# Linear attention and channel mix on one core: q transposed by DMA instead of PE, a v cast moved to ScalarE, a two-term mix rewritten as a difference, a factor moved into a relu, and loads gated

## The chip, the cores and the metric

The kernel runs on one core of a Trainium2 chip. The metric is device time in microseconds (us) per execution. Most executions of one kernel agree within about one per cent; a run over 1.5% above the fastest of its kernel is called slow and is left out of the comparisons. All profile readings are of one execution per kernel. PE is the matmul engine, PEld its weight load, DVE the VectorE, ACT the ScalarE, POOL the GpSimd; SP only issues DMAs here.

## The reference, cut to what matters

```python
# q, k, v: (8 batches, 8 heads, 576 rows, 64)
q_s = softmax(q, axis=-1)                    # over the head dimension
k_s = softmax(k, axis=2)                     # over the sequence
kv  = einsum('bhsd,bhse->bhde', k_s, v)
x   = einsum('bhsd,bhde->bhse', q_s, kv)     # then heads joined: (8, 576, 512)
x_prev = x shifted by one row, zero first
xk = mu_k * x + (1 - mu_k) * x_prev
xr = mu_r * x + (1 - mu_r) * x_prev
out = sigmoid(xr @ w_r) * (relu(xk @ w_k)**2 @ w_v)
```

## The kernel before: the parts that matter

The work comes in two interleaved streams. `attention(b, g)` handles one half batch (four heads) and leaves `xk` and `xr` for it; there are 16 half batches. `unit(n)` handles 384 rows of the channel mix: 32 matmuls `kfp` (with wk), then three times four `rp` (with wr) and eight `vp` (with wv); there are 12 units. A scheduler has fixed the order of each engine's instructions at build time, so it need not be the order of the source. In the traces below, work that is ready stands behind an earlier instruction of the same engine that still waits (13.7 us of PE's idle time before 44.0 us come from one such case on DVE).

```python
def emit_weights():                       # POOL issues these; the DMA casts f32 to bf16
    ...                                   # wk in four loads, wr in four
    for h in range(2):                    # wv in two, halved in place by DVE
        nc.gpsimd.dma_start(out=wv_h, in_=ap)
        nc.vector.tensor_scalar(out=wv_h, in0=wv_h, scalar1=0.5, scalar2=None, op0=ALU.mult)

def attention(b, g):
    nc.gpsimd.tensor_copy(out=vv[...], in_=t[:, 2, ...])          # v cast on POOL
    for i in (1, 0):                                              # exp of k, then of q
        nc.scalar.activation(out=eqk[:, i, ...], in_=t[:, i, ...], func=ACT.Exp)
    nc.vector.reduce_sum(out=rsum[:], ...); nc.vector.reciprocal(out=rrec[:], ...)
    nc.vector.tensor_tensor(out=qs[...], in0=eq, in1=rrec..., op=ALU.mult)   # normalised q
    ...                                   # kvp: 18 matmuls; w: scaled and masked kv
    for j in range(J):                    # J = 9
        nc.tensor.transpose(out=qtp[:, j // 8, j % 8, :], in_=qs[:, j, :], identity=ident[:])
    nc.vector.tensor_copy(out=qt[...], in_=qtp[...])              # PSUM to SBUF
    for hf in range(2):
        ...                               # xp: two matmuls of w with qt
        nc.scalar.copy(out=xb[:, hf, ...], in_=xp[...])
    nc.vector.tensor_copy(out=xb[:, :, 1:64], in_=xb[:, :, 576:639])   # the shifted column
    for m, dst in enumerate((xk, xr)):
        for hf in range(2):
            nc.vector.tensor_scalar(out=xm[:, hf, :], in0=xb[now], scalar1=mu[...], op0=ALU.mult)
            nc.vector.tensor_scalar(out=xq[:, hf, :], in0=xb[prev], scalar1=om[...], op0=ALU.mult)
        nc.vector.tensor_tensor(out=dst[...], in0=xm[:], in1=xq[:], op=ALU.add)
```

(Access patterns and some arguments are cut, marked by `...`.)

The softmax here doesn't subtract the row's maximum and nothing guards it: scores larger than these inputs give would overflow.

Of the kernel before, what the change touches and what calls it, by code (L numbers as in the profile page):

```python
# [8 lines left out]
ACT = mybir.ActivationFunctionType  # L9
ALU = mybir.AluOpType  # L10
AX = mybir.AxisListType

F32 = mybir.dt.float32
BF16 = mybir.dt.bfloat16


@with_exitstack
def kernel(
# [18 lines left out]
    nc = tc.nc  # L37

    B, H, S, D = q.shape
# [18 lines left out]

    raw = {}

    def emit_load(b: int, g: int):
        t = ldpool.tile([128, 3, 2, J * D], F32, tag="raw", name="raw")
        for i, src in enumerate((q, k, v)):
            ap = bass.AP(tensor=src.tensor,
                         offset=src.offset + (b * H + 4 * g) * S * D,
                         ap=[[J * D, 128], [2 * S * D, 2], [1, J * D]])
            nc.sync.dma_start(out=t[:, i, :, :], in_=ap)
        raw[b, g] = t

    mu_sb = const.tile([8, 128], F32, name="mu_sb")  # L70
    for m, src in enumerate((moe_mu_k, moe_mu_r)):
        for g in range(2):
# [1 line left out]
                         ap=[[64, 2], [128, 2], [1, 64]])  # L74
            nc.scalar.dma_start(out=mu_sb[4 * m + 2 * g:4 * m + 2 * g + 2, :]
                                .rearrange("p (u e) -> p u e", u=2), in_=ap)
    emit_load(0, 0)
    emit_load(0, 1)


# [18 lines left out]
    wv_bf = const.tile([128, FT, C], BF16, name="wv_bf")  # L99
    wr_bf = const.tile([128, CT, C], BF16, name="wr_bf")  # L100

    def emit_weights():
        for dst, src, n in ((wk_bf, moe_w_k, F), (wr_bf, moe_w_r, C)):
            for g in range(2):
                for u in range(2):
                    ap = bass.AP(tensor=src.tensor,
                                 offset=src.offset + (4 * g + 2 * u) * D * n,
                                 ap=[[n, 64], [D * n, 2], [1, n]])
                    nc.gpsimd.dma_start(out=dst[64 * u:64 * u + 64, 2 * g:2 * g + 2, :],
                                        in_=ap)  # L110
        for h in range(2):
            n = FT // 2
            ap = bass.AP(tensor=moe_w_v.tensor,
                         offset=moe_w_v.offset + h * n * 128 * C,
                         ap=[[C, 128], [128 * C, n], [1, C]])
            wv_h = wv_bf[:, h * n:(h + 1) * n, :]
            nc.gpsimd.dma_start(out=wv_h, in_=ap)
            nc.vector.tensor_scalar(out=wv_h, in0=wv_h, scalar1=0.5, scalar2=None,  # L118
                                    op0=ALU.mult)

    mu = const.tile([128, 8], F32, name="mu")
    om = const.tile([128, 8], F32, name="om")

    def emit_mu():
        mup = psum.tile([128, 8], F32, tag="mm", bufs=4, name="mup")
        nc.tensor.transpose(out=mup[:], in_=mu_sb[:], identity=identf[:])
        nc.vector.tensor_copy(out=mu[:], in_=mup[:])
        nc.vector.tensor_scalar(out=om[:], in0=mup[:], scalar1=-1.0, scalar2=1.0,
                                op0=ALU.mult, op1=ALU.add)


    xpair = {}
# [2 lines left out]
    def attention(b: int, g: int):  # L135
        t = raw.pop((b, g))
        vv = vvs[box[0] % 3]
        xb = xbs[box[0] % 3]
        box[0] += 1
        if b // 2 not in xpair:  # L140
            xpair[b // 2] = (xpool.tile([128, CT, 2 * S], BF16, tag="xk", name="xk"),
                             xpool.tile([128, CT, 2 * S], BF16, tag="xr", name="xr"))
        xk, xr = xpair[b // 2]
        c0 = S * (b % 2)

        nc.gpsimd.tensor_copy(out=vv[:, :, 0:128].rearrange("p j (u d) -> p j u d", u=2),  # L146
                              in_=t[:, 2, :, :].rearrange("p u (j d) -> p j u d", d=D))
        eqk = apool.tile([128, 2, J, 2, D], BF16, tag="eqk", name="eqk")
        for i in (1, 0):
            nc.scalar.activation(  # L150
                out=eqk[:, i, :, :, :],
                in_=t[:, i, :, :].rearrange("p u (j d) -> p j u d", d=D),
                func=ACT.Exp)
        eq = eqk[:, 0, :, :, :].rearrange("p j u d -> p (j u) d")
        rsum = apool.tile([128, 2 * J], F32, tag="rsum", name="rsum")
        nc.vector.reduce_sum(out=rsum[:], in_=eq, axis=AX.X)  # L156
        rrec = apool.tile([128, 2 * J], F32, tag="rrec", name="rrec")
        nc.vector.reciprocal(out=rrec[:], in_=rsum[:])
        qs = apool.tile([128, J, 128], BF16, tag="qs", name="qs")
        nc.vector.tensor_tensor(out=qs[:].rearrange("p j (u d) -> p (j u) d", u=2),  # L160
                                in0=eq, in1=rrec[:, :, None].to_broadcast((128, 2 * J, D)),
                                op=ALU.mult)
        yield
        kvp = psum.tile([128, 2, 512], F32, tag="att", bufs=2, name="kvp")
        for j in range(J):
            for hf in range(2):
                r = slice(64 * hf, 64 * hf + 64)
                nc.tensor.matmul(kvp[:, hf, 0:129],  # L168
                                 lhsT=eqk[r, 1, j, :, :].rearrange("p u d -> p (u d)"),
                                 rhs=vv[r, j, 0:129], start=(j == 0), stop=(j == J - 1))  # L170
        rz = apool.tile([128, 2], F32, tag="rz", name="rz")
        nc.vector.reciprocal(out=rz[:], in_=kvp[:, :, 128])
        w = apool.tile([128, 2, 128], BF16, tag="w", name="w")
        for hf in range(2):
            nc.vector.scalar_tensor_tensor(out=w[:, hf, :], in0=kvp[:, hf, 0:128],  # L175
                                           scalar=rz[:, hf:hf + 1], in1=mask[:],
                                           op0=ALU.mult, op1=ALU.mult)
        yield
        qtp = psum.tile([128, 2, 8, 128], BF16, tag="att", bufs=2, name="qtp")
        qt = apool.tile([128, 2, S], BF16, tag="qt", name="qt")  # L180
        for j in range(J):
            nc.tensor.transpose(out=qtp[:, j // 8, j % 8, :], in_=qs[:, j, :],  # L182
                                identity=ident[:])
        nc.vector.tensor_copy(  # L184
            out=qt[:, :, :].rearrange("p h (j c) -> p j h c", c=64),
            in_=qtp[:].rearrange("p a j c -> p (a j) c")[:, 0:J, :]
            .rearrange("p j (h c) -> p j h c", h=2))
        yield
        for hf in range(2):
            xp = psum.tile([128, 2, 512], F32, tag="att", bufs=2, name="xp")  # L190
            for a in range(2):
                nc.tensor.matmul(xp[:, a, 0:288], lhsT=w[:, hf, :],  # L192
                                 rhs=qt[:, hf, 288 * a:288 * a + 288],
                                 start=True, stop=True)
            nc.scalar.copy(out=xb[:, hf, 64:64 + S].rearrange("p (a c) -> p a c", a=2),
                           in_=xp[:, :, 0:288])
            if hf == 0:
                yield
        nc.vector.tensor_copy(out=xb[:, :, 1:64], in_=xb[:, :, 64 + 512:64 + 512 + 63])
        yield  # L200
        for m, dst in enumerate((xk, xr)):
            xm = apool.tile([128, 2, S], BF16, tag="xm", name="xm")
            xq = apool.tile([128, 2, S], BF16, tag="xq", name="xq")
            for hf in range(2):
                c = 4 * m + 2 * g + hf
                nc.vector.tensor_scalar(out=xm[:, hf, :], in0=xb[:, hf, 64:64 + S],  # L206
                                        scalar1=mu[:, c:c + 1], scalar2=None, op0=ALU.mult)
                nc.vector.tensor_scalar(out=xq[:, hf, :], in0=xb[:, hf, 0:S],  # L208
                                        scalar1=om[:, c:c + 1], scalar2=None, op0=ALU.mult)
            nc.vector.tensor_tensor(out=dst[:, 2 * g:2 * g + 2, c0:c0 + S],  # L210
                                    in0=xm[:], in1=xq[:], op=ALU.add)
            yield


    def unit(n: int):
# [3 lines left out]
        for fc in range(FT):  # L219
# [3 lines left out]
                                 rhs=xk[:, ct, c0:c0 + U],  # L223
                                 start=(ct == 0), stop=(ct == CT - 1))
            rel = mpool.tile([128, U], BF16, tag="rel", bufs=3, name="rel")
            nc.scalar.activation(out=rel[:], in_=kfp[:, 0:U], func=ACT.Relu)  # L226
            nc.vector.tensor_tensor(out=k2[:, fc, :], in0=rel[:], in1=rel[:], op=ALU.mult)
            yield
        for m in range(U // 128):
# [24 lines left out]
            pass  # L254


    a0 = attention(0, 0)
    next(a0)
    a1 = attention(0, 1)
    next(a1)  # L260
    emit_weights()
    emit_mu()
    emit_load(1, 0)
    emit_load(1, 1)
    for gen in (a0, a1):
        drain(gen)

    def attention_of(batches):
        for b in batches:
            for g in range(2):  # L270
                if b + 1 < B:
                    emit_load(b + 1, g)
                yield from attention(b, g)

    ASTEPS = 16
# [45 lines left out]
```

## Time and profile before

The median is 246.6 us over three runs. The profiled execution has a span of 244.5 us.

| stretch (us) | what bounds it | sign in the profile |
|---|---|---|
| 20 to 44 | DVE's order, waiting for wv | PE 3.3 us busy of 24, DVE 10.2, DMA share 1.11 |
| 45 to 190 | DVE | DVE busy 141.4 of 145 us, PE 130.9 |
| 190 to 244.5 | PE | attention is over; a unit is 12.95 us of back-to-back matmuls |

From the page of the kernel before, the busy time per engine, and the rows of the table of 40 equal slices (each digit is a busy share in tenths):

```profile
PE 190.5 (78%) x1296; PEld 103.2 (42%) x1313; DVE 186.2 (76%) x434; ACT 120.0 (49%) x197; POOL 33.8 (14%) x32
PE   0335200898987969797979999979999999999992
DVE  1489312999999999999999999999969844252521
DMA  6999999921997587898881303203113031322313
```

PE has a hole in slices 5 to 7, while the DMA engines are full. From there on DVE is at 9 for most of the way; PE reaches a steady 9 only when DVE drops.

The chain of waits of the kernel before, the pieces around that hole (columns: start in us, us, what):

```profile
13.97 2.21 POOL vv_104 L146
...
16.72 2.37 POOL wr_bf L109 x4
19.09 0.70 POOL wv_bf L117
19.79 21.27 DMA wv_bf<-in_moe_w_v_dram
41.09 0.69 DVE wv_bf L118
...
43.28 0.68 DVE xk L210
44.00 3.49 PE kfp L222 x11
```

Read it backwards: the first `kfp` matmuls that need the second half of batch 0 wait for `xk`; the mix that makes it is queued on DVE behind the halving of wv; that waits 21 us for wv to land; and POOL issued wv only from 19.1 us on, because v casts stand in front of it in POOL's order (experiments 7 and 9 test both steps).

The timeline of the kernel before beside one v cast, from DVE and from POOL:

```profile
21.59 0.36 DVE L206 TENSOR_SCALAR xm<-xb_102,mu 128x576 bf16<-128x576 bf16 x1
21.87 1.25 DVE L208 TENSOR_SCALAR xq<-xb_102,om 128x576 bf16<-128x576 bf16 x1
...
21.68 1.28 POOL L146 CAST vv_108<-raw 128x1152 bf16<-128x1152 f32 x1 [1.08 <-DMA raw<-in_v_dram]
```

A DVE scaling of this shape takes 0.36 us and, beside a POOL cast, 1.25 us.

### The profile page before, as it was taken

How to read it: one execution, taken by the hardware profiler on the slowest of the kernel's cores; microseconds unless marked ns; L12 is line 12 of the kernel's file. 1: busy time of each engine (PE TensorE's matmuls, PEld its weight loads, DVE VectorE, ACT ScalarE, POOL GpSimd, SP SyncE). 2: the span in 40 equal slices, each digit the busy share in tenths (PEclk: the TensorE clock that was granted, in tenths of full speed). 3: DMA queues.
4: the chain of work that ended last, by engine and by line, in shares of the span. 5: the costliest groups of instructions: out<-in, count | busy, mean ns of one | idle time of the engine just before them, and what ended most of it. 6: DMA issues, size and time to landing. Idle time of an engine off the chain costs nothing.

```text
span 244.5 us, 3656 instructions
## 1 busy us (share of the span) xinstructions
PE 190.5 (78%) x1296; PEld 103.2 (42%) x1313; DVE 186.2 (76%) x434; ACT 120.0 (49%) x197; POOL 33.8 (14%) x32
## 2 busy tenths in 40 slices
PE   0335200898987969797979999979999999999992
PEld 0223200453543545453544555534655545454540
DVE  1489312999999999999999999999969844252521
ACT  4351520495292755465383774741734626162620
POOL 2375011610112010110110140100000000000000
PEclk9999655699999999999999999999999999999997
DMA  6999999921997587898881303203113031322313
GB/s 224 368 319 314 298 293 357 394 86 25 254 333 292 130 315 230 252 298 268 260 285 44 86 3 79 51 4 86 43 39 92 0 90 43 73 55 51 81 43 86
DMA packets 21065, 40.60 MB, mean 166 GB/s; under 512 B 2104, under 2 KB 3640, under 8 KB 21048
## 3 DMA queue, kind: packets, MB, share of 16 engines
q1 hardware_dynamic: 18816, 37.76, 49.4%
q0 software_dynamic: 2208, 2.62, 6.1%
q8 instruction: 10, 0.16, 0.3%
q14 instruction: 7, 0.06, 0.1%
q10 hardware_dynamic: 24, 0.00, 0.0%
HBM read 33.56 MB, written 9.44 MB: 176 GB/s over the span
## 4 chain that ended last, share of the span: by engine, by line
PE 49%; DVE 27%; DMA 14%; ACT 4%; POOL 2%; issue 1%; DVEq 0%; ACTq 0%
PE vp L239 21%; PE kfp L222 14%; PE rp L232 9%; DMA wv_bf<-in_moe_w_v_dram 9%; DVE qs L160 5%; DVE xq L208 4%; DMA raw<-in_v_dram 4%; DVE xm L206 3%; PE xp L192 2%; DVE xr L210 2%; DVE xk L210 2%; DVE rsum L156 2%; DVE ot L242 2%; ACT eqk L150 2%; PE qtp L182 2%; DMA raw<-in_q_dram 2%
## 5 line engine op out<-in xcount | busy, mean ns | idle before, releaser
L222 PE MATMUL kfp<-xk,wk_bf 128*128 128x384 bf16 x384 | 69.4, 331 | 15.9 <-DVE xk L210 15.1
L226 ACT ACTIVATE rel<-kfp 128x384 bf16<-128x384 f32 x96 | 46.1, 495 | 38.0 <-PE kfp L222 32.5
L222 PEld LDWEIGHTS <-wk_bf 128*128 128x128 bf16 x384 | 37.3, 99 | 40.0 <-issue 16.9
L150 ACT ACTIVATE eqk<-raw 128x1152 bf16<-128x1152 f32 x32 | 36.7, 1163 | 34.5 <-DMA raw<-in_q_dram 15.1
L242 DVE SCALAR_TENSOR_TENSOR ot<-th,vp 128x512 f32<-128x512 f32 x36 | 24.5, 684 | 21.7 <-PE vp L239 18.6
L235 ACT ACTIVATE th<-rp 128x512 f32<-128x512 f32 x36 | 21.6, 599 | 33.8 <-PE rp L232 33.5
L232 PE MATMUL rp<-wr_bf,xr 128*128 128x512 bf16 x130 | 36.4, 379 | 0.7
L156 DVE TENSOR_REDUCE rsum<-eqk 128x18 f32<-128x1152 bf16 x16 | 21.5, 1345 | 8.5 <-ACT eqk L150 8.5
L160 DVE TENSOR_TENSOR qs<-eqk,rrec 128x1152 bf16<-128x1152 bf16 x16 | 21.6, 1351 | 0.1
L192 PE MATMUL xp<-qt,w 128*128 128x288 bf16 x64 | 12.1, 295 | 10.2 <-DVE qt L184 6.8
L232 PEld LDWEIGHTS <-xr 128*128 128x128 bf16 x144 | 13.7, 98 | 13.3
L182 PE MATMUL qtp<-ident,qs 128*128 128x128 bf16 x144 | 11.6, 231 | 5.0 <-DVE qs L160 4.8
L146 POOL CAST vv_100<-raw 128x1152 bf16<-128x1152 f32 x6 | 8.2, 1371 | 49.3 <-PE kvp L168 42.2
L146 POOL CAST vv_108<-raw 128x1152 bf16<-128x1152 f32 x5 | 10.8, 2164 | 27.6 <-PE kvp L168 16.9
L168 PEld LDWEIGHTS <-eqk 64*128 64x128 bf16 x288 | 9.6, 102 | 11.0 <-issue 5.1
L146 POOL CAST vv_104<-raw 128x1152 bf16<-128x1152 f32 x5 | 7.7, 1547 | 44.3 <-DMA raw<-in_v_dram 22.8
L182 PEld LDWEIGHTS <-qs 128*128 128x128 bf16 x144 | 9.4, 103 | 9.5 <-DVE qs L160 7.6
L192 PEld LDWEIGHTS <-w 128*128 128x128 bf16 x64 | 6.2, 98 | 17.1 <-DVE w L175 7.4
L210 DVE TENSOR_TENSOR xr<-xm,xq 128x1152 bf16<-128x1152 bf16 x16 | 12.7, 794 | 0.0
L210 DVE TENSOR_TENSOR xk<-xm,xq 128x1152 bf16<-128x1152 bf16 x16 | 12.1, 754 | 0.0
L184 DVE COPY qt<-qtp 128x1152 bf16<-128x1152 bf16 x16 | 12.0, 747 | 0.0
L118 DVE TENSOR_SCALAR wv_bf<-wv_bf 128x2048 bf16<-128x2048 bf16 x2 | 1.4, 694 | 13.1 <-DMA wv_bf<-in_moe_w_v_dram 13.1
(78 smaller groups left out, 244.8 us busy)
## 6 DMA issues: line engine op xcount, KB each, us to landing
raw<-in_q_dram SPq DMA_DIRECT2D x16, 576.0 KB, 7.6
raw<-in_k_dram SPq DMA_DIRECT2D x16, 576.0 KB, 7.9
raw<-in_v_dram SPq DMA_DIRECT2D x16, 576.0 KB, 8.5
out_dram<-ot SPq DMA_DIRECT2D x72, 128.0 KB, 2.4
wk_bf<-in_moe_w_k_dram POOLq DMA_DIRECT2D x4, 256.0 KB, 6.8
wv_bf<-in_moe_w_v_dram POOLq DMA_DIRECT2D x2, 512.0 KB, 18.9
wr_bf<-in_moe_w_r_dram POOLq DMA_DIRECT2D x4, 128.0 KB, 8.8
mu_sb<-in_moe_mu_k_dram ACTq DMA_DIRECT2D x2, 1.0 KB
```

The source lines that it names most:

```text
L146: nc.gpsimd.tensor_copy(out=vv[:, :, 0:128].rearrange("p j (u d) -> p j u d", u=2), in_=t[:, 2, :, :].rearrange("p u (j d) -> p j u d", d=D))
L150: nc.scalar.activation(out=eqk[:, i, :, :, :], in_=t[:, i, :, :].rearrange("p u (j d) -> p j u d", d=D), func=ACT.Exp)
L156: nc.vector.reduce_sum(out=rsum[:], in_=eq, axis=AX.X)
L160: nc.vector.tensor_tensor(out=qs[:].rearrange("p j (u d) -> p (j u) d", u=2), in0=eq, in1=rrec[:, :, None].to_broadcast((128, 2 * J, D)), ...
L182: nc.tensor.transpose(out=qtp[:, j // 8, j % 8, :], in_=qs[:, j, :], identity=ident[:])
L192: nc.tensor.matmul(xp[:, a, 0:288], lhsT=w[:, hf, :], rhs=qt[:, hf, 288 * a:288 * a + 288], start=True, stop=True)
L210: nc.vector.tensor_tensor(out=dst[:, 2 * g:2 * g + 2, c0:c0 + S], in0=xm[:], in1=xq[:], op=ALU.add)
L222: nc.tensor.matmul(kfp[:, 0:U], lhsT=wk_bf[:, ct, fc * 128:(fc + 1) * 128], rhs=xk[:, ct, c0:c0 + U], start=(ct == 0), stop=(ct == CT - 1))
L226: nc.scalar.activation(out=rel[:], in_=kfp[:, 0:U], func=ACT.Relu)
L232: nc.tensor.matmul(rp[:], lhsT=xr[:, ct, c0 + 128 * m:c0 + 128 * m + 128], rhs=wr_bf[:, ct, :], start=(ct == 0), stop=(ct == CT - 1))
L239: nc.tensor.matmul(vp[:], lhsT=k2[:, ft, 128 * m:128 * m + 128], rhs=wv_bf[:, ft, :], start=(ft == 0), stop=(ft == FT - 1))
L242: nc.vector.scalar_tensor_tensor(out=ot[:], in0=th[:], scalar=1.0, in1=vp[:], op0=ALU.add, op1=ALU.mult)
```

## The change

Five things are changed. The normalised q goes through a DMA transpose, which frees PE of 144 transposes and DVE of 16 copies out of PSUM. The v cast goes from POOL to ACT. The mix is written as x_prev + mu * (x - x_prev), with `om` gone. The 0.5 of wv becomes a factor sqrt(0.5) in the relu's scale, which the square turns into 0.5. One weight load is made to wait for the first raw loads; the q loads of batch 1's two half batches wait for wk and for wr, and that of batch 2's first half for wv (this last line is not in the cut below).

```diff
+HALF_ROOT = 0.5 ** 0.5
-    def emit_load(b: int, g: int):
+    def emit_load(b: int, g: int, gate=None):
...
-            nc.sync.dma_start(out=t[:, i, :, :], in_=ap)
+            ld = nc.sync.dma_start(out=t[:, i, :, :], in_=ap)
+            after(ld, gate)          # ld waits for the DMA `gate`
+            gate = None              # so only the q load is gated
...
-            nc.vector.tensor_scalar(out=wv_h, in0=wv_h, scalar1=0.5, ...)
...
-        nc.gpsimd.tensor_copy(out=vv[...], in_=t[:, 2, ...])
-        for i in (1, 0):
+        for i in (0, 1):
             nc.scalar.activation(out=eqk[:, i, ...], ..., func=ACT.Exp)
+        nc.scalar.copy(out=vv[...], in_=t[:, 2, ...])
...
-        for j in range(J):
-            nc.tensor.transpose(out=qtp[...], in_=qs[:, j, :], identity=ident[:])
-        nc.vector.tensor_copy(out=qt[...], in_=qtp[...])
+        qt = apool.tile([128, J, 128], BF16, tag="qt", name="qt")
+        nc.sync.dma_start_transpose(out=qt[:], in_=qs[:].rearrange("p j c -> p (j c)"))
...
-            for a in range(2):       # xp in two matmuls of 288 columns
+            for c, e in ((0, 8), (8, J)):      # now 512 and 64 columns
...
+        nc.vector.tensor_tensor(out=xd[:], in0=xb[now], in1=xb[prev], op=ALU.subtract)
...
-                xm = x * mu ; xq = x_prev * om        # two tensor_scalar
+                xm = xd * mu                          # one
-            dst = xm + xq
+            dst = xm + x_prev
...
-            nc.scalar.activation(out=rel[:], in_=kfp[:, 0:U], func=ACT.Relu)
+            nc.scalar.activation(out=rel[:], in_=kfp[:, 0:U], func=ACT.Relu, scale=HALF_ROOT)
...
+    wdone = emit_weights(first)      # its first weight load waits for raw v of half batch (0,0)
+    emit_load(1, 0, wdone[3])        # behind wk
+    emit_load(1, 1, wdone[7])        # behind wr
```

(The lines of the mix are abbreviated, and the comments are added here.)

More of the change, by code (lines that the diff above doesn't have):

```diff
@@ L59, with after @@
     raw = {}
-    def emit_load(b: int, g: int):
+    SYNC = mybir.DependencyInfo(mybir.DependencyClass.Sync, mybir.DependencyReason.DATA)
+    def after(later, earlier):
+        if earlier is not None:
+            tc.add_manual_dep(later.ins, earlier.ins.name, SYNC)
+    def emit_load(b: int, g: int, gate=None):
         t = ldpool.tile([128, 3, 2, J * D], F32, tag="raw", name="raw")
@@ L66, in emit_load @@
                          ap=[[J * D, 128], [2 * S * D, 2], [1, J * D]])
-            nc.sync.dma_start(out=t[:, i, :, :], in_=ap)
+            ld = nc.sync.dma_start(out=t[:, i, :, :], in_=ap)
+            after(ld, gate)
+            gate = None
         raw[b, g] = t
+        return ld
     mu_sb = const.tile([8, 128], F32, name="mu_sb")
@@ L76 @@
                                 .rearrange("p (u e) -> p u e", u=2), in_=ap)
-    emit_load(0, 0)
+    first = emit_load(0, 0)
     emit_load(0, 1)
@@ L100, with emit_weights @@
     wr_bf = const.tile([128, CT, C], BF16, name="wr_bf")
-    def emit_weights():
+    def emit_weights(gate):
+        done = []
         for dst, src, n in ((wk_bf, moe_w_k, F), (wr_bf, moe_w_r, C)):
@@ L108, in emit_weights @@
                                  ap=[[n, 64], [D * n, 2], [1, n]])
-                    nc.gpsimd.dma_start(out=dst[64 * u:64 * u + 64, 2 * g:2 * g + 2, :],
-                                        in_=ap)
+                    done.append(nc.gpsimd.dma_start(
+                        out=dst[64 * u:64 * u + 64, 2 * g:2 * g + 2, :], in_=ap))
+                    after(done[-1], gate)
+                    gate = None
         for h in range(2):
@@ L116, in emit_weights @@
             wv_h = wv_bf[:, h * n:(h + 1) * n, :]
-            nc.gpsimd.dma_start(out=wv_h, in_=ap)
-            nc.vector.tensor_scalar(out=wv_h, in0=wv_h, scalar1=0.5, scalar2=None,
-                                    op0=ALU.mult)
+            done.append(nc.gpsimd.dma_start(out=wv_h, in_=ap))
+        return done
     mu = const.tile([128, 8], F32, name="mu")
-    om = const.tile([128, 8], F32, name="om")
     def emit_mu():
@@ L127, in emit_mu @@
         nc.vector.tensor_copy(out=mu[:], in_=mup[:])
-        nc.vector.tensor_scalar(out=om[:], in0=mup[:], scalar1=-1.0, scalar2=1.0,
-                                op0=ALU.mult, op1=ALU.add)
     xpair = {}
@@ L144, in attention @@
         c0 = S * (b % 2)
-        nc.gpsimd.tensor_copy(out=vv[:, :, 0:128].rearrange("p j (u d) -> p j u d", u=2),
-                              in_=t[:, 2, :, :].rearrange("p u (j d) -> p j u d", d=D))
         eqk = apool.tile([128, 2, J, 2, D], BF16, tag="eqk", name="eqk")
-        for i in (1, 0):
+        for i in (0, 1):
             nc.scalar.activation(
@@ L153, in attention @@
                 func=ACT.Exp)
+        nc.scalar.copy(out=vv[:, :, 0:128].rearrange("p j (u d) -> p j u d", u=2),
+                       in_=t[:, 2, :, :].rearrange("p u (j d) -> p j u d", d=D))
         eq = eqk[:, 0, :, :, :].rearrange("p j u d -> p (j u) d")
@@ L178, in attention @@
         yield
-        qtp = psum.tile([128, 2, 8, 128], BF16, tag="att", bufs=2, name="qtp")
-        qt = apool.tile([128, 2, S], BF16, tag="qt", name="qt")
-        for j in range(J):
-            nc.tensor.transpose(out=qtp[:, j // 8, j % 8, :], in_=qs[:, j, :],
-                                identity=ident[:])
-        nc.vector.tensor_copy(
-            out=qt[:, :, :].rearrange("p h (j c) -> p j h c", c=64),
-            in_=qtp[:].rearrange("p a j c -> p (a j) c")[:, 0:J, :]
-            .rearrange("p j (h c) -> p j h c", h=2))
+        qt = apool.tile([128, J, 128], BF16, tag="qt", name="qt")
+        nc.sync.dma_start_transpose(out=qt[:], in_=qs[:].rearrange("p j c -> p (j c)"))
         yield
         for hf in range(2):
-            xp = psum.tile([128, 2, 512], F32, tag="att", bufs=2, name="xp")
-            for a in range(2):
-                nc.tensor.matmul(xp[:, a, 0:288], lhsT=w[:, hf, :],
-                                 rhs=qt[:, hf, 288 * a:288 * a + 288],
+            xp = psum.tile([128, 1024], F32, tag="att", bufs=2, name="xp")
+            for c, e in ((0, 8), (8, J)):
+                nc.tensor.matmul(xp[:, 64 * c:64 * e], lhsT=w[:, hf, :],
+                                 rhs=qt[:, c:e, 64 * hf:64 * hf + 64],
                                  start=True, stop=True)
-            nc.scalar.copy(out=xb[:, hf, 64:64 + S].rearrange("p (a c) -> p a c", a=2),
-                           in_=xp[:, :, 0:288])
+            nc.scalar.copy(out=xb[:, hf, 64:64 + S], in_=xp[:, 0:S])
             if hf == 0:
@@ L200, in attention @@
         yield
+        xd = apool.tile([128, 2, S], BF16, tag="xd", name="xd")
+        nc.vector.tensor_tensor(out=xd[:], in0=xb[:, :, 64:64 + S], in1=xb[:, :, 0:S],
+                                op=ALU.subtract)
         for m, dst in enumerate((xk, xr)):
             xm = apool.tile([128, 2, S], BF16, tag="xm", name="xm")
-            xq = apool.tile([128, 2, S], BF16, tag="xq", name="xq")
             for hf in range(2):
                 c = 4 * m + 2 * g + hf
-                nc.vector.tensor_scalar(out=xm[:, hf, :], in0=xb[:, hf, 64:64 + S],
+                nc.vector.tensor_scalar(out=xm[:, hf, :], in0=xd[:, hf, :],
                                         scalar1=mu[:, c:c + 1], scalar2=None, op0=ALU.mult)
-                nc.vector.tensor_scalar(out=xq[:, hf, :], in0=xb[:, hf, 0:S],
-                                        scalar1=om[:, c:c + 1], scalar2=None, op0=ALU.mult)
             nc.vector.tensor_tensor(out=dst[:, 2 * g:2 * g + 2, c0:c0 + S],
-                                    in0=xm[:], in1=xq[:], op=ALU.add)
+                                    in0=xm[:], in1=xb[:, :, 0:S], op=ALU.add)
             yield
@@ L225, in unit @@
             rel = mpool.tile([128, U], BF16, tag="rel", bufs=3, name="rel")
-            nc.scalar.activation(out=rel[:], in_=kfp[:, 0:U], func=ACT.Relu)
+            nc.scalar.activation(out=rel[:], in_=kfp[:, 0:U], func=ACT.Relu,
+                                 scale=HALF_ROOT)
             nc.vector.tensor_tensor(out=k2[:, fc, :], in0=rel[:], in1=rel[:], op=ALU.mult)
@@ L260 @@
     next(a1)
-    emit_weights()
     emit_mu()
-    emit_load(1, 0)
-    emit_load(1, 1)
+    emit_load(1, 0, wdone[3])
+    emit_load(1, 1, wdone[7])
     for gen in (a0, a1):
@@ L271, in attention_of @@
                 if b + 1 < B:
-                    emit_load(b + 1, g)
+                    emit_load(b + 1, g, wdone[-1] if b == 1 and g == 0 else None)
                 yield from attention(b, g)
```

## The prediction

> **What bounds the kernel now.** Three stretches, by the table of busy time per window. (1) 20 to 44 us: PE is busy 3.3 of 24 us, DVE 10.2. The chain of waits goes through the landing of wv (21.3 us of DMA, to 41.1), then the in-place halving of wv on DVE, then the mix of the second half of batch 0, and only at 44.0 does the first unit's matmul stream restart. DVE runs in order, so the halving, which waits for wv, holds back work that was ready. (2) 45 to 190 us: DVE is busy 141.4 of 145 us, PE 130.9, ACT 83. DVE bounds. (3) 190 to 244.5: attention is over and PE bounds; a unit takes 12.95 us in the chain of waits, and about 53 us of such work follow the last xp matmul (192).
>
> **What changes.**
> DVE, back-to-back costs from the chain of waits: four xq scalings go (0.28 us each), the qt copy goes (0.67), one subtraction comes (1152 elements, two bf16 inputs, like the xk addition: 0.67). Net -1.1 us per half batch, -18 us over 16; the wv halving goes (-1.4). POOL's v casts go (33.8 us POOL busy): an xq takes 0.36 us at the median but 1.25 at most, as at 21.9 us beside a v cast; I estimate some 9 us of the 186 DVE us are such waits. DVE: 186 to about 158.
> PE: the 16x9 transposes go (0.5 to 0.67 us per nine, about -9 us); xp moves the same columns.
> ACT: 16 v casts, estimated from the exp of the same shape at 1.16: +18.6 us, 120 to 139.
> DMA: 16 transposes of 295 KB each. No run shows their cost. The Trainium skill ("DMA: Bandwidth & Descriptors", Latency and other measured facts) has 261 GB/s for a transpose: 1.1 us and the fixed latency; its "VectorE: DVE Perf Modes" (The three transpose paths) has 1.3 us for one 128x128 block, so at worst nearly 12 us for nine. I estimate 2 to 4 us of all 16 engines, and 4 to 8 us from issue to landing, as they queue behind loads (which now take 7.6 to 8.5). In the new program order DVE has about 8 us of other work between qs and the xb copy that needs its transpose, so most is hidden.
> Start: weights wait for the first load, and most of batch 1's loads for wk. First raws and wk are about 6.8 MB; at the 315 GB/s of 20 to 44 us they are in by about 22 us, so the full unit can start near 25 instead of 44.
>
> **Sum.** DVE needs about 140 us up to the last xp; some 10 are done by 25 us. 25 + 130/0.96 = 160, and 53 us of PE-bound work follow: 213. ACT at about 80% and PE near 90% of that stretch, and exposed transpose latency, cost something: 218 us, 205 to 238. All of the start and nearly all of the DVE saving lie on the critical path; the PE saving lies mostly off it.
>
> Chances: faster by over 2% 0.88, within 2% 0.06, slower 0.06.
>
> **What would show it.** Continuous kfp matmuls from about 25 us; no DVE wait for wv; DVE near 158 busy and no xq-like op at 1.25 us; POOL nearly idle; last xp near 160; last 50 us unchanged; the transposes landing in under 8 us; few PE waits for qt.
>
> **What would make it wrong.** Transposes that hold the DMA engines 8 us or more each, or that block the one issuing queue in front of the loads: PE xp then waits for qt and exp for raw, DMA share goes to 1, and the kernel gets slower. A start where the gate delays batch 1, so DVE starves at 25 to 40 us.

## The result and the profile after

The changed kernel takes 229.77 us (228.96 to 231.07, four runs), with a span of 228.1 us in the profile. Its ratio to the kernel before is 0.928, 95% interval 0.921 to 0.936. A ratio here is the mean time of one kernel's fast runs over that of the other's in the same rounds, so it is not quite the ratio of the medians. The result is correct.

The busy times and the same rows of the page after:

```profile
PE 182.5 (80%) x1153; PEld 92.8 (41%) x1169; DVE 160.1 (70%) x367; ACT 136.0 (60%) x213; POOL 7.1 (3%) x16
PE   0100055599989989979999999999999999999991
DVE  0550077899989999799999999995867843343521
DMA  6999999999799999999899899444041140414114
```

DVE lost 26 us of work, and POOL nearly all of its own. The first slices are not better than before, though: PE and DVE are both at 0 in slices 4 and 5 (counted from 1), and PE is in full flow from slice 9. The DMA engines are now all but full from slice 2 to slice 25.

The table of busy time per window, after, for the last part of the start, the middle and the tail:

```profile
20.00:44.00 24.00, 8.26 (x58) 4.39 (x58) 11.85 (x26) 10.86 (x13) 0.00 (x0) 0.91 1.11 274
44.00:175.00 131.00, 124.85 (x835) 63.10 (x846) 120.08 (x276) 94.81 (x154) 0.00 (x0) 0.99 0.83 227
175.00:228.00 53.00, 47.81 (x245) 24.06 (x247) 21.15 (x47) 20.92 (x41) 0.00 (x0) 0.99 0.26 60
```

(After the window and its length, the columns are the busy us of PE, PEld, DVE, ACT and POOL with the number of instructions, the granted PE clock, the DMA share, GB/s.) In the middle PE is now busy 95% and DVE 92%: PE leads, no longer DVE.

The chain of waits of the kernel after, the pieces that answer to the ones shown of before:

```profile
13.72 1.27 DVE qs L169
...
15.26 9.87 SPq L189
25.22 0.53 SPq L74
25.81 0.98 SPq L74
26.88 9.15 DMA raw<-in_q_dram
...
42.33 4.00 PE kfp L223 x12
```

The wait for wv is gone, and another has taken its place: SP's queue holds the second DMA transpose (L189) for 9.87 us, and the raw loads of batch 1 stand behind it. The `kfp` stream that was held up to 44.0 us now starts at 42.3.

The instructions and waits of the transposed tile `qt`, after, and PE's largest wait from the list of waits (us in total, times, longest us):

```profile
L189 SPq DMA_TRANSPOSE qt<-qs x16: 1273/1475/10114, 8.8 to 147.6; - x16
DMA to landing us min/median/max: 3.2/3.8/16.5
PE xp L194 <- DMA qt<-qs: 17.0, 2, 16.2
```

A typical transpose is issued in 1.5 us and lands 3.8 us after issue. The first two take far longer: the second, issued at 15.0 us, lands 16.5 us later, and the first costs PE 16.2 us in one wait, as it is issued at 8.8 us and its `xp` starts at 28.2.

So three numbers describe each kernel: **A**, when the first matmuls that need both halves of batch 0 start (the full `kfp` stream); **B**, when the last `xp` starts; and the tail after B. The tail is 52.2 to 53.1 us in every profile that is used here. B is read from the view of the tile `xp` (count, ns of the shortest, the median and the longest one, first and last start in us), before and after:

```profile
L192 PE MATMUL xp<-qt,w x64: 282/286/448, 16.2 to 192.0; 128*128 128x288 bf16 x64
L194 PE MATMUL xp<-qt,w x64: 190/316/631, 28.2 to 175.5; 128*128 128x512 bf16 x32, 128*128 128x64 bf16 x32
```

| kernel | A | B | B - A | span |
|---|---|---|---|---|
| before | 44.0 | 192.0 | 148.0 | 244.5 |
| changed | 42.3 | 175.5 | 133.2 | 228.1 |
| as predicted | 25 | 160 | 135 | 213 (218 us foretold with a margin) |

Nearly the whole gain lies in the middle (14.8 of 16.5 us at B), and the length of the middle came as foretold. Nearly all of the gain expected at the start is missing.

### The profile page after: what moved, and what is told of

Its sections match the earlier page's. It is cut to its first block, busy times and chain, and to the rows that moved or that the text cites. A ratio compares the mean times of both kernels' runs of the same rounds, so it can differ in the third digit from the quotient of the medians.

```text
span 228.1 us, 3352 instructions
## 1 busy us (share of the span) xinstructions
PE 182.5 (80%) x1153; PEld 92.8 (41%) x1169; DVE 160.1 (70%) x367; ACT 136.0 (60%) x213; POOL 7.1 (3%) x16
## 3 DMA queue, kind: packets, MB, share of 16 engines
q1 hardware_dynamic: 37760, 42.48, 66.8%
## 4 chain that ended last, share of the span: by engine, by line
PE 53%; DVE 18%; DMA 14%; SPq 7%; ACT 3%; issue 2%; DVEq 0%
PE vp L241 21%; PE kfp L223 19%; PE rp L234 10%; DMA raw<-in_q_dram 8%; SPq L189 5%; DMA raw<-in_k_dram 4%; DVE qs L169 3%; DVE rsum L165 3%; PE xp L194 2%; DVE xm L209 2%; DMA qt<-qs 2%; PE kvp L177 2%; DVE xd L203 2%; ACT eqk L157 2%; DVE xk L211 1%
## 5 line engine op out<-in xcount | busy, mean ns | idle before, releaser
L223 PE MATMUL kfp<-xk,wk_bf 128*128 128x384 bf16 x384 | 71.2, 336 | 7.0 <-DVE xk L211 6.4
L194 PE MATMUL xp<-qt,w 128*128 128x512 bf16 x64 | 13.4, 306 | 18.3 <-DMA qt<-qs 17.0
L209 DVE TENSOR_SCALAR xm<-xd,mu 128x576 bf16<-128x576 bf16 x64 | 20.7, 367 | 0.1
L194 PEld LDWEIGHTS <-w 128*128 128x128 bf16 x64 | 5.8, 103 | 25.6 <-issue 15.5
L177 PE MATMUL kvp<-vv_100,eqk 64*128 64x129 bf16 x108 | 4.9, 232 | 10.4 <-ACT vv_100 L161 10.4
L197 ACT CAST xb_102<-xp 128x576 bf16<-128x576 f32 x12 | 7.6, 647 | 7.8 <-PE xp L194 7.8
L200 DVE COPY xb_102<-xb_102 128x126 bf16<-128x126 bf16 x6 | 1.2, 194 | 15.2 <-ACT xb_102 L197 15.2
L184 DVE SCALAR_TENSOR_TENSOR w<-kvp,rz,mask 128x128 bf16<-128x128 f32 x32 | 9.7, 342 | 0.2
L197 ACT CAST xb_110<-xp 128x576 bf16<-128x576 f32 x10 | 6.4, 639 | 4.6 <-PE xp L194 4.5
L161 ACT CAST vv_100<-raw 128x1152 bf16<-128x1152 f32 x6 | 7.0, 1167 | 1.5 <-DMA raw<-in_v_dram 1.5
L241 PE MATMUL vp<-wv_bf,k_961 128*128 128x512 bf16 x24 | 6.0, 380 | 1.7 <-DVE k_961 L229 1.7
L161 ACT CAST vv_108<-raw 128x1152 bf16<-128x1152 f32 x5 | 5.8, 1161 | 2.3 <-DMA raw<-in_v_dram 2.3
```

What stands on the lines that cost most here:

```text
L177: nc.tensor.matmul(kvp[:, hf, 0:129], lhsT=eqk[r, 1, j, :, :].rearrange("p u d -> p (u d)"), rhs=vv[r, j, 0:129], start=(j == 0), stop=(j ...
L194: nc.tensor.matmul(xp[:, 64 * c:64 * e], lhsT=w[:, hf, :], rhs=qt[:, c:e, 64 * hf:64 * hf + 64], start=True, stop=True)
L209: nc.vector.tensor_scalar(out=xm[:, hf, :], in0=xd[:, hf, :], scalar1=mu[:, c:c + 1], scalar2=None, op0=ALU.mult)
L223: nc.tensor.matmul(kfp[:, 0:U], lhsT=wk_bf[:, ct, fc * 128:(fc + 1) * 128], rhs=xk[:, ct, c0:c0 + U], start=(ct == 0), stop=(ct == CT - 1))
L241: nc.tensor.matmul(vp[:], lhsT=k2[:, ft, 128 * m:128 * m + 128], rhs=wv_bf[:, ft, :], start=(ft == 0), stop=(ft == FT - 1))
```

## The experiments

**Theory T.** The start is lost to the first two DMA transposes, which are starved; elsewhere the DMA transposes pay. **Rivals**: the start would be late anyway (R), and the transposes gain nothing in the middle. For the slow first transposes there are three candidates: the casting weight loads on the other queue (W), raw loads issued before them on the same queue (B), or a cold start of the first such instruction (C).

### 1. PE transposes for the first two half batches

```diff
+        if b == 0:
+            qtp = psum.tile([128, 2, 8, 128], BF16, tag="att", bufs=2, name="qtp")
+            ...                                   # nine PE transposes
+            nc.vector.tensor_copy(out=qt[:], in_=qtp[...])
+        else:
             nc.sync.dma_start_transpose(out=qt[:], ...)
```

> The changed kernel, but the two half batches of batch 0 are transposed on PE with a PSUM copy; the other 14 still by DMA. Theory T (the whole shortfall is the start: the two first DMA transposes land only after 16 us, while 14 later ones take 3.8): the first full run of kfp matmuls starts near 25 to 30 us instead of 42.3, and the time falls from 229.8 to about 213 to 219 us. Rival R (the start would be late anyway, because wk or the second half batch is not there before 40 us, or because DMA transposes throttle the middle): kfp starts near 40 and the time stays within 2% of 229.8.

Measured: 224.25 us, ratio 0.906 (0.901 to 0.912). A is 36.1, B 168.6. T is right about the cause and wrong about the size: 5.5 us came back, not 11 to 17. The stream starts 6 us sooner, not 12 to 17. What holds it now is in the timeline of ACT in this run:

```profile
27.44 1.16 ACT L157 ACTIVATE eqk<-raw 128x1152 bf16<-128x1152 f32 x1 [5.49 <-DMA raw<-in_q_dram]
30.48 1.16 ACT L157 ACTIVATE eqk<-raw 128x1152 bf16<-128x1152 f32 x1 [1.88 <-DMA raw<-in_k_dram]
31.55 1.16 ACT L204 CAST xb<-xp 128x576 bf16<-128x576 f32 x2
```

The `xp` of half batch (0,1) was there at 25.6 us, but its copy `xb` stands on ACT behind two exps of batch 1, which wait for raw loads. Experiments 5 and 6 go into this.

### 2. PE transposes for all 16

```diff
-        nc.sync.dma_start_transpose(out=qt[:], in_=qs[:].rearrange("p j c -> p (j c)"))
+        qtp = psum.tile(...)                      # nine PE transposes and a DVE copy, as above
```

> The changed kernel with all 16 transposes on PE and a PSUM copy by DVE, so every part of the change but the DMA transposes. Theory T (DMA transposes pay in the middle, where DVE is 92% busy, and cost only at the start): DVE busy rises by about 16 x 0.67 = 11 us to 171, PE by 9; the start is early as in the run with PE for the first two; time about 219 to 226 us, slower than that one, by 4 to 10 us. Rival R (DMA transposes gain nothing in the middle): as fast as, or faster than, the run with PE for the first two.

Measured: 230.3 us, ratio 0.930 (0.925 to 0.935), on the same chip and in the same rounds as experiment 1: 6 us slower than with DMA transposes for the last 14. A is 35.7 and B 176.4, so B - A is 140.7 against 132.5. DVE is busy 170.0 us against 161.1. T holds. The views of `xp` in 1 and 2:

```profile
L201 PE MATMUL xp<-qt,w x64: 190/318/615, 16.1 to 168.6; 128*128 128x512 bf16 x32, 128*128 128x64 bf16 x32
L198 PE MATMUL xp<-qt,w x64: 190/318/615, 15.7 to 176.4; 128*128 128x512 bf16 x32, 128*128 128x64 bf16 x32
```

Together, 1 and 2 show that the DMA transposes in the whole change give 6 us in the middle and take about as much at the start: with or without all of them, the time is 230 us.

### 3 and 4. Why the first two are slow: weights later; all batch 1 loads later

```diff
-    wdone = emit_weights(first)                   # 3: every weight load waits
+    wdone = emit_weights(tr[0, 1])                #    for the second DMA transpose
```

> The changed kernel, but all weight loads (the casting queue) wait for the second DMA transpose of batch 0 to land. Theory W (the casting weight loads on the other queue starve the transposes): the two first transposes land within 8 us of issue, and the xp of half batch 0 runs before 20 us instead of at 28.2. Rival C (the first transposes are slow because they are first, a cold start): they still take over 12 us. Rival B (they wait behind raw loads issued before them on the same queue): between the two, about 8 to 12 us, as six loads are still ahead. Total time is not the point; the weights come later, so kfp may not start earlier than 40 us.

```diff
             after(ld, gate)
-            gate = None                           # 4: k and v are gated as q is
```

> The changed kernel, but all three loads of batch 1's first half wait for wk and all three of its second half for wr, not only q: the two loads (k and v) that were let through ahead of the transposes now come after them. Theory B (a backlog of raw loads in front of the transposes on the same queue): the transposes land some 3 to 4 us sooner (two loads of 576 KB at about 330 GB/s), kfp starts near 38, time some 3 us less. Theory W (casting weight loads) or C (cold start): the transposes still take about 14 us or more and the time stays within 1% of 229.8.

Experiment 3 measured 230.3 us (ratio 0.931, two runs). The first `xp` starts at 14.9 us and that of the second transpose, issued at 14.0, at 17.4. From its timeline and its list for `qt`:

```profile
17.37 1.18 PE L195 MATMUL xp<-qt,w 128*128 128x512 bf16 x4 [0.42 <-DMA qt<-qs]
...
26.64 4.17 PE L224 MATMUL kfp<-xk,wk_bf 128*128 128x384 bf16 x24 [0.36 <-DMA wk_bf<-in_moe_w_k_dram]
...
DMA to landing us min/median/max: 3.2/6.0/8.0
```

No transpose takes over 8.0 us, the first included: there is no cold start, and C falls. The full `kfp` stream starts at 26.6 us, almost where the prediction had put it; the expectation had allowed for 40 at the earliest, and was wrong in that. Yet the time does not get better: PE then waits for wv up to 38.6 us, and the second unit, which needs batch 1, starts its main stream at 60.7 us, as in the changed kernel (60.5).

Experiment 4 measured 227.5 us in its three fast runs (226.2 to 228.2), ratio 0.919 (0.913 to 0.925). That overlaps with the interval of the changed kernel, so a gain in time is not shown. Its profiled run was slow (232.4 us), so its times are to be read with reserve: the first `xp` waits until 21.9 us instead of 28.2, the second until 29.2. Two raw loads fewer in front are worth about 6 us to the first transpose (B), yet both transposes still take 13 to 15 us from issue to use. In experiment 3 it is 6 or less, with the same six raw loads issued before the first transpose and one more before the second; what differs is that the weights are out of the way (W). Both W and B act. From issue to use, the first transpose takes 19.4 us in the changed kernel, 13.2 in 4 and 5.9 in 3; the second takes 20.3 (it had landed after 16.5), 14.6 and 3.4. So W is the larger, above all for the second; how large B is rests on the slow run.

The Trainium skill ("DMA: Bandwidth & Descriptors", Issuing engines are not separate DMA queues) says that DMAs of all issuing engines run on the same 16 DMA engines and interleave. These runs agree: loads issued by POOL delayed transposes issued by SP. The same page (Queues, rings and completion order) says that each DMA engine takes turns between queues packet by packet. The trace agrees. From the DMA view (packets, MB, share of 16 engines; q0 carries the weights, q1 all that SP issues), the changed kernel from 21 to 23 us, with transposes and weights under way:

```profile
q0 software_dynamic: 329, 0.30, 88.7%
q1 hardware_dynamic: 336, 0.09, 31.1%
```

And experiment 3 from 15 to 17 us, with a transpose under way and no weights:

```profile
q1 hardware_dynamic: 1210, 0.35, 97.4%
```

Beside the weights, one packet of SP's queue goes for each weight packet, and in 2 us 336 of them go instead of 1210. An estimate: a transpose of 1152 packets of 256 bytes then takes 1152 / 168 per us = 7 us, and two take 14, instead of 2 us each. Most of the rest of the 19.4 us is the raw loads in front: packets under 512 bytes, the size of a transpose's, are few before 19 us (35 from 17 to 19 us, 223 in the next 2 us).

### 5 and 6. The rest of the start: the q load freed; ACT's order changed

Both start from experiment 1.

```diff
-    emit_load(1, 0, wdone[3])
+    emit_load(1, 0)                               # 5
```

> The run with PE transposes for batch 0 (224.3 us), and the q load of batch 1's first half no longer waits for wk. In that run ScalarE, which runs in order, held two exps of batch 1's first half, waiting for raw q and k that were issued only at 20.5 us, in front of the xb copies of half batch (0,1), which ran at 31.6 though their xp was there at 25.6. Theory G (the gate on q makes the late start that is left): q lands near 18, the xb copies run near 26 to 27, the full kfp stream starts near 30 instead of 36, the time falls to about 217 to 221 us. Rival D (the DMA engines are the limit of the start, so moving q forward pushes wk or wr and wv back by the same bytes): kfp or rp or vp then wait for weights and the time stays within 2 us of 224.3.

```diff
+            if b == 1 and g == 0:                 # 6: these exps stay behind the xb copies of (0,1)
+                tc.add_manual_dep(ex.ins, xbc[0, 1].ins.name, ...)
```

> The run with PE transposes for batch 0, loads unchanged, but the exps of batch 1's first half are ordered behind the xb copies of half batch (0,1) on ScalarE. Theory O (ScalarE's order, not the data, is what delays the full kfp stream): it starts near 30 instead of 36, as in the run that frees q; the time falls by 2 to 6 us. Rival D (DMA supply): kfp starts earlier but the next unit starves for batch 1's raws, and the time stays within 2 us of 224.3.

Experiment 5 gave a ratio of 0.910 (0.903 to 0.917) in its fast runs (225.7 and 227.3 us); two runs were slow, among them the profiled one at 405.9 us, with PE busy for 373 us. Its profile says nothing about the kernel and isn't used. Experiment 6 gave 226.3 us, ratio 0.909 (0.903 to 0.915). Neither beats experiment 1, so the rival D stands (for 5 by its time alone). The profile of experiment 6 shows where the lead was lost. The timeline of PE in 6, then in 1:

```profile
30.01 1.46 PE L234 MATMUL kfp<-xk,wk_bf 128*128 128x384 bf16 x4
...
54.92 3.41 PE L234 MATMUL kfp<-xk,wk_bf 128*128 128x384 bf16 x20 [2.38 <-DVE xk L222]
```

```profile
36.06 2.72 PE L230 MATMUL kfp<-xk,wk_bf 128*128 128x384 bf16 x8 [2.68 <-DVE xk L218]
...
54.87 4.24 PE L230 MATMUL kfp<-xk,wk_bf 128*128 128x384 bf16 x25 [0.53 <-DVE xk L218]
```

The first unit starts 6 us sooner in 6, but the second unit, which needs batch 1, starts its main stream at 54.9 us in both. In the changed kernel that was at 60.5, and these 5.6 us match the 5.5 us that experiment 1 gained. The DMA share is 1.0 or more from 10 to 50 us in both: the data of batch 1 is the next limit. Experiment 3 agrees: its first unit is the earliest of all (26.6), and its second starts at 60.7. So an early first unit, by itself, is worth nothing beyond this point. Whether another order of loads could bring batch 1 forward was not tried.

### 7 to 10. Each part alone, on the kernel before

```diff
-            nc.vector.tensor_scalar(out=wv_h, ..., scalar1=0.5, ...)     # 7
-            nc.scalar.activation(out=rel[:], in_=kfp[:, 0:U], func=ACT.Relu)
+            nc.scalar.activation(out=rel[:], in_=kfp[:, 0:U], func=ACT.Relu, scale=0.5 ** 0.5)
```

> The kernel before with one part alone: no halving of wv on DVE, its 0.5 as a scale of the relu. My theory of the start of before (DVE's order: the halving at 35.5 and 41.1 us waits for wv and holds back the mix of half batch (0,1)): the full kfp stream starts near 32 instead of 44, time 235 to 240. Rival (DMA supply bounds the start): kfp starts earlier, but units stall for rp, vp weights or raws up to about 44, and the time falls by less than 4 us, to 243 or more.

```diff
+        xd = x - x_prev                                                 # 8: the mix of the change
```

> The kernel before with one part alone: the mix by difference (four scalings fewer, one subtraction more per half batch). DVE-bound middle: DVE busy falls from 186 to about 179 (16 x 0.45 us), the time by about the same, 5 to 8 us, to 239 to 242. Rival (PE sets the pace behind it, 131 of 145 us busy): under 3 us.

```diff
-        nc.gpsimd.tensor_copy(out=vv[...], in_=...)                     # 9
-        for i in (1, 0):
+        for i in (0, 1):
...
+        nc.scalar.copy(out=vv[...], in_=...)
```

> The kernel before with one part alone: the v cast on ScalarE instead of GpSimd (and the exp of q before that of k, as in the change). My sum had 9 us of DVE time lost beside the GpSimd casts: DVE busy falls from 186 to about 177 and, as DVE bounds the middle, the time by 4 to 9 us, to 238 to 243. Rival (ScalarE gets 19 us more and its order then delays others, or the lost DVE time is not on the chain): DVE busy falls as said, but the time stays within 2% of before.

```diff
-        nc.tensor.transpose(...) x9 and the copy of qtp                 # 10
+        nc.sync.dma_start_transpose(out=qt[:], in_=...)                 #     with xp in 512 and 64
```

> The kernel before with one part alone: all 16 transposes by DMA. Theory (pays in the DVE-bound middle, costs at the start, where they queue behind twelve raw loads and the weights): the first xp waits for its transpose until 30 us or later, the full kfp stream starts 3 to 8 us later than at 44; the middle gets about 11 us shorter; time 2 to 8 us less, 240 to 246. Rival (no cost at the start, because the start waits for wv anyway): 234 to 238.

| on the kernel before | time (us) | ratio, interval | A | B | B - A | DVE busy |
|---|---|---|---|---|---|---|
| nothing | 246.6 to 249.0 | 1 | 44.0 | 192.0 | 148.0 | 186.2 |
| 7: relu scale | 238.3 | 0.957 (0.951 to 0.962) | 32.2 | 183.7 | 151.5 | 185.4 |
| 8: mix by difference | 241.1 | 0.969 (0.965 to 0.974) | 44.3 | 187.6 | 143.3 | 179.1 |
| 9: v cast on ACT | 233.6 | 0.942 (0.937 to 0.947) | 37.6 | 178.2 | 140.6 | 176.8 |
| 10: DMA transposes | 234.9 | 0.947 (0.941 to 0.954) | 46.9 | 180.2 | 133.3 | 171.0 |

Seven is as expected: DVE no longer waits for wv, A comes 11.8 us sooner, and 8.3 us of that are left at B. Eight is as expected too.

Nine gained more than the 4 to 9 us foretold. DVE busy fell by 9.4 us, as the prediction's sum had it, but A also came 6.5 us sooner. The cause is in POOL's timeline in experiment 9:

```profile
4.08 2.40 POOL L109 DMA_DIRECT2D wr_bf<-in_moe_w_r_dram  x4
8.03 0.77 POOL L117 DMA_DIRECT2D wv_bf<-in_moe_w_v_dram  x1 [1.55 <-DMA wk_bf<-in_moe_w_k_dram]
```

In the kernel before, POOL issued wv only from 19.1 us on, because v casts stand in front of it in POOL's order. With the v casts out of its queue, POOL issues wv from 8.0 us on, not from 19.1, and the second halving, which stood at 41.1 us, runs at 31.3.

Ten gained 13 us: my theory had at most 8, and the time lies in the rival's range, though not for the rival's reason. Its start is as bad as foretold, with the first `xp` at 36.2 us. From PE's timeline in experiment 10:

```profile
36.22 1.12 PE L185 MATMUL xp<-qt,w 128*128 128x512 bf16 x4 [24.82 <-DMA qt<-qs]
...
46.92 4.96 PE L214 MATMUL kfp<-xk,wk_bf 128*128 128x384 bf16 x15 [1.39 <-DVE xk L202]
```

But the kernel before was waiting until 44.0 anyway, so this costs 2.9 us and not 25. And the middle is 14.7 us shorter, not 11: DVE busy falls by 15.2 us, of which the copies out of PSUM were 12.0.

### 11 and 12. Two parts together, and six half batches on PE

Eleven has the edits of 7 and 8 together. Twelve is experiment 1 with `if b < 3` in place of `if b == 0`.

> The kernel before with two parts: 0.5 in the relu scale, and the mix by difference. Alone they gave ratios 0.957 and 0.969 to before; if they add up (one acts on the start, the other on the DVE-bound middle), the ratio is about 0.927 and the time about 230 us, as much as the whole change. Rival (they overlap, because once DVE is relieved PE or the loads bind): 0.94 or more.

> The changed kernel with PE transposes for batches 0 to 2 (six half batches) and DMA transposes for the other ten: a try for a faster kernel. If DMA supply still limits up to about 60 us, the four transposes more that are taken off the DMA engines (2 us of all 16 each) free loads: 2 to 5 us faster than with two on PE (ratio to before 0.885 to 0.899). Rival (after 40 us PE and DVE limit, so each of the four costs 0.5 to 0.7 us of both): 1 to 3 us slower than it (ratio 0.91 to 0.92).

Eleven measured 236.5 us, ratio 0.954 (0.948 to 0.959): no more than the relu scale alone is shown to give. The time is in the rival's range (0.94 or more), so by the ratios the parts don't add up. Why is not shown. Its B - A is 147.3 us, with DVE busy 59.8 of the 60 us from 80 to 140, but 9 and 10 fill DVE as much there (59.9 and 60.0) with a shorter middle. And in the single profiles the gains at B nearly do add: 8.3 and 4.4 us alone, 11.7 together; but the profile of 8 is of its slowest run and that of 11 of its fastest.

Twelve measured 225.3 us, ratio 0.910 (0.905 to 0.915), against 0.906 for experiment 1: not a gain, and too close to call a loss. Experiment 1 is the fastest version measured, at 224.25 us; its interval does not touch that of the changed kernel.

### Why the middle stops at 133 us

Experiment 10 alone has B - A of 133.3, the whole change 133.2, and experiment 1 132.5. All of the DVE time that the mix and the v cast save on top buys nothing there. An estimate of PE's own floor, from the chain of waits: from A to B lie nine units of 12.95 us less the last 7.8 us of the ninth, and 14 half batches with 0.63 us of `kvp` and 0.65 of `xp`: 116.6 - 7.8 + 17.9 = 126.7 us. With nine PE transposes of 0.50 us for each half batch it is 133.7. The kernels with DMA transposes stand at 132.5 to 133.3, those with PE transposes and a relieved DVE (2 and 9) at 140.6 and 140.7: each 6 to 7 us above its floor. (Experiments 6 and 12 have 140.4 and 135.4; 6 stalls for batch 1, as shown, and 12 has six sets of PE transposes.) The kernel before stands 14 us above its floor, since DVE bound it. The busy times from A to B support this. PE is busy 127.9 us in 10, 127.0 in the changed kernel and 127.0 in 1, but 133.8 in 9 and 134.9 in 2. DVE is busy 127.2, 121.8, 122.0, 136.3 and 130.9. The length of the middle goes with PE, and 5 us less of DVE work change nothing. Experiments 10 and 2 have almost the same DVE work in all (171.0 and 170.0 us), and 10, without PE transposes, has the middle 7.4 us shorter. Once DVE is relieved, what counts is PE. Why all of them stay 6 to 7 us above the floor is not shown.

## Why the prediction was right or wrong, point by point

The time of 229.8 us lies in the stated range of 205 to 238, and "faster by over 2%" came true. The central 218 us was 12 us too low, by one term of the sum: the start came 17 us later than foretold, of which the margin of 5 us covered a part. That the time lies in the range is owed to the width of the range.

- **"The full unit can start near 25 instead of 44"**: this is the term that was mis-sized. It started at 42.3, so 1.7 us of the expected 19 came. The sum counted when the bytes would be in, 6.8 MB by 22 us. It left out what else the first `xp` needs: a DMA transpose, issued just when the DMA engines are fullest. Experiment 3 shows the transposes quick once weights wait; experiment 1 shows 5.5 us come back with PE transposes for batch 0. The other 6 us or so never were to be had by these means: with all of the first unit early (experiments 6 and 3), the second still waits for batch 1, until 54.9 and 60.7 us.
- **"4 to 8 us from issue to landing"**, "most is hidden": about right for the 14 later ones (median of all 3.8 us; PE waited 17.0 us in total, 16.2 of it for the first). It was taken as one number for all 16. What failed is that an average cost was used where the first instance matters.
- **"2 to 4 us of all 16 engines"** for a transpose: 2.1 us, from the share of the SP queue with and without them (66.8% of 228.1 us in the changed kernel, 52.1% of 228.7 in experiment 2; the difference is 33 us over 16).
- **DVE 186 to about 158**: 160.1. The slow scalings beside POOL casts are gone: the new scalings take 0.362 to 0.373 us, all 64 of them. DVE no longer waits for wv. **ACT 139**: 136.0. **POOL nearly idle**: 7.1.
- **"The PE saving lies mostly off" the critical path**: wrong. With DVE relieved, PE sets the pace, and taking the transposes off PE and the copies off DVE is worth 6 us of time (experiment 2 against 1). The DVE savings overlap instead: one large one (2 or 9) already comes within 7 us of PE's floor.
- **Sum of the middle, 135 us; tail, 53 us**: 133.2 and 52.6. For the middle this is partly luck: the 135 us were 130 us of DVE work at 96%, but DVE had 121.8 us there, and what set the length was PE, with 127.0.
- **"A start where the gate delays batch 1"**: named as a risk, and half seen. The gate held only the q load, and the scheduler put k and v of the same half batch in front of it, at 4.9 and 5.9 us. So they stood in front of the transposes, while q, issued at 25.2, came last. Gating all three (experiment 4) let the first `xp` run 6 us sooner (in a slow run), but no clear gain in time came of it.
- Not foreseen at all: a v cast in POOL's queue also delays the weight loads that POOL issues (experiment 9).

## What to carry to other kernels

Price a DMA that takes the place of on-chip work for its first use as well as its typical one: at the start the DMA engines are full with loads, and a small transfer that everything waits for gets only its share; a mixed version (PE at first, DMA later) was the fastest measured here. When several parts relieve the same engine, don't add their gains: compute the floor of the next engine and stop counting there. Before crediting an earlier start, look at whether the second unit of work can start earlier too.

## What the Trainium skill lacked or had wrong

- "DMA: Bandwidth & Descriptors" (Latency and other measured facts) gives 261 GB/s for a DMA transpose with a non-contiguous middle dimension, and 350 to 400 for the contiguous case. Here a 128x1152 bf16 transpose from SBUF to SBUF (294,912 bytes) used 2.1 us of all 16 engines, 1.9 by experiment 10 against the kernel before: about 140 to 160 GB/s. The profile counts 1184 packets for each; 1152 of 256 bytes would carry the data. The measurement decides.
- "VectorE: DVE Perf Modes" (The three transpose paths) gives 1309 ns by DMA and 390 ns on TensorE for one 128x128 block. For nine blocks in one go the runs show 3.8 us from issue to landing by DMA (the median of the changed kernel; 5.0 and 6.0 in experiments 1 and 3), and 0.50 us on PE back to back, plus a 0.75 us DVE copy out of PSUM. Per block, neither figure scales.
- No page that was read gives, in time on this chip, what a transpose of this size costs on the issuing queue: the runs show 1.3 to 3.3 us of SP's queue as a rule, and 10.1 and 14.4 us when the DMA engines were behind (the changed kernel and experiment 10).
- No page that was read gives the delay of a transpose next to casting weight loads from the other queue: 13 to 24 us from issue to use with them and raw loads in front (24 in experiment 10), 6 us or less without the weights.
